# Mamba2 scan and SiLU MLP on one core: the second product of the first units in seven segments, and the sums of g's blocks moved from GpSimd to DMA and VectorE

## The chip, the cores and the metric

The kernel runs on one core of a Trainium2 chip. The metric is device time in microseconds (us) of one execution; the median of eight runs is what a change is judged by. A profile of one execution is at hand, with every instruction of every engine.

## The reference, cut to what matters

The inputs are `x` (4, 8, 768, 32), `a` (4, 8, 768), `B` and `C` (4, 8, 768, 16), and the weights `w_in` (256, 2048) and `w_out` (2048, 256), all float32.

```python
# block 1, for each batch and head: a state-space scan
y[i] = sum over j <= i of (C_i . B_j) * exp(cum_i - cum_j) * x_j + (C_i . state) * decay_i
# bridge: (batch, head, seq, dim) -> (3072 tokens, 256)
X = y.transpose(0, 2, 1, 3).reshape(3072, 256)
# block 2
h = X @ w_in          # (3072, 2048)
g = h * sigmoid(h)    # SiLU
out = g @ w_out       # (3072, 256)
```

The two large products, `X @ w_in` (the first) and `g @ w_out` (the second), hold most of the arithmetic.

## The kernel before, in words

The 3072 tokens are cut in 12 units of 256 tokens, three for each batch. For each unit the scan makes a transposed X (tile `XM`), the first product and SiLU make `g` (tile `gT`, 128 partitions x 16 blocks x 256 tokens, four buffers in `gpool`), and the second product reads `g` and `w_out`. All products are float32, and each 128x128 by 128x256 product is two TensorE instructions in the trace. There is no scheduler: engines carry out their instructions in the order in which the code emits them, and that order is written out by hand.

Two ways of doing the products stand side by side.

- Units 0 to 3 do the first product plainly: `f_s1(g, j)`, called for j = 0 to 7, makes two of the 16 blocks of `g` by four products and one SiLU on ScalarE.
- From unit 4 on, units are taken in pairs (`G` = 2 to 5, units 2G and 2G + 1), and `f_x1(G, j, ...)` does the first product of the pair with seven products in place of eight, the Strassen-Winograd way. It needs sums of blocks of `w_in` (`f_SW`, four tiles, each from one instruction on GpSimd) and sums of blocks of X (`f_XT`, four for each pair, on GpSimd).

The second product likewise. `s2_list` does it plainly for units 0 and 1: 64 products, with `g` as the weights that TensorE holds. `s2_pair(P)` does pairs 1 to 5 in seven segments of eight products, called "1", "w", "5", "6", "7", "4" and "3" and done in that order. Pair P's `g` is four blocks: b11 and b21 are the even and the odd blocks of unit 2P, b12 and b22 those of unit 2P + 1. Each segment accumulates in a PSUM tile `o_ps`, of which there is one buffer (`ps_o`, bufs=1); ScalarE copies it to a tile `ps` (`ppool`, five buffers), GpSimd adds such tiles (`p_add`), VectorE transposes the sum and SyncE's queue writes it out (`f_out`, called a round later through the list `PEND`). In the last pair VectorE takes GpSimd's additions, and every other segment uses a buffer of `hp` instead.

Segments "5", "6", "7" and "4" need sums of blocks: `f_TS(P, i, ...)` makes TN = b12 - b11 (in a tile of its own), then in place b11 = b22 - TN, b12 = b22 - b12 and b21 = b21 - b11. All are on GpSimd, in instructions of 128x256, other than two of the four sums of the last pair. `f_SO` makes the sums of blocks of `w_out` on VectorE.

`f_s2(n)` emits the next n products of the second product, whichever unit or pair they belong to. It is called between the products of the first one, so that the two alternate on TensorE: four products of each in turn in units 2 and 3, and from unit 4 on one "s" of the string `ORDER[j]` at a time, for example

```python
ORDER = ("W15s6sss7sss43", "W1s56ss7sss43s", ...
```

The scan of later units is emitted in between by `scan_piece` (pieces T, E, B, C, D, G, S, Y; S is `f_SW`) and by `scan_plan`. Piece G ends in small products on TensorE (`f_D0`, `f_G0`) followed by VectorE's `f_S` and `f_M` and ScalarE's `f_SM`; piece Y is further small products (`f_Y`) and ScalarE's copy of them to `XM` (`f_X`).

At the start the arriving weights are worked over in pieces (`w_size` on ScalarE, `w_bits` on VectorE and GpSimd; pieces b13 to b15 fall in unit 2), and `busy(n, small)` has TensorE multiply zeros, n products of 512 columns and `small` products of 64 columns.

Of the kernel before, what the change touches and what calls it, by code (L numbers as in the profile page):

```python
# [21 lines left out]
def kernel(  # L22
# [219 lines left out]
    busy(4, 14)  # L242
# [230 lines left out]


    def f_s1(g, j):
        if j == 0:
            GTS[g] = gpool.tile([128, NF, UT], FP32, name="gT")
        xm = XM[g].rearrange("p (w c) t -> p w (c t)", w=2)
        hp = ps_h.tile([128, 2, UT], FP32, name="hp")
        for i in range(2):  # L480
            f = 2 * j + i
            for kc in range(KC):
                nc.tensor.matmul(out=hp[:, i], lhsT=w_in_sb[:, kc, f * 128:(f + 1) * 128],  # L483
                                 rhs=xm[:, kc], start=(kc == 0), stop=(kc == KC - 1))
        nc.scalar.activation(GTS[g][:, 2 * j:2 * j + 2], hp, AF.Silu)  # L485
        if j == 7:
            XM.pop(g)


    def s2_list(units):  # L490
        for g in units:
            b, t0 = at(g)
            r = out[b * S + t0:b * S + t0 + UT].rearrange("(k c i) m -> k i c m", k=2, c=2)
            o = ps_o.tile([128, 2, d_model], FP32, name="o_ps")
            for c in range(2):
                for f in range(NF):
                    nc.tensor.matmul(out=o[:, c], lhsT=GTS[g][:, f, 128 * c:128 * c + 128], rhs=w_out_sb[:, f, :],  # L497
                                     start=(f == 0), stop=(f == NF - 1), skip_group_check=True)
                    if f == NF - 1 and c == 1:
                        for e in range(2):  # L500
                            o_sb = ppool.tile([128, UT], FP32, name="ps")
                            nc.scalar.activation(o_sb, o[:, e], AF.Copy)
                            for k in range(2):
                                nc.sync.dma_start(out=r[k][:, e], in_=o_sb[64 * k:64 * k + 64])
                    yield

# [3 lines left out]
    SO, TN, PEND = [], {}, []  # L510

    def f_SO(i):

        def lo(t):
            return t[:, 0:4], t[:, 4:8]

        def new():
            if i == 3:
                return lo(spare(None, 128))
            return [wtp.tile([128, 2, WF], FP32, name=n).rearrange("p a (b m) -> p (a b) m", m=128)  # L520
                    for n in ("wu", "wv")]

        SO.append(new())
        b = lambda k, m: lo(wjo[:, k, m])
        a0, a1, op = ((b(0, 1), b(1, 1), ALU.add), (SO[0], b(0, 0), ALU.subtract),
                      (b(0, 0), b(0, 1), ALU.subtract), (b(1, 0), SO[min(i, 1)], ALU.subtract))[i]
        for e in range(2):
            nc.vector.tensor_tensor(out=SO[i][e], in0=a0[e], in1=a1[e], op=op)

    def gb(P, k, v):  # L530

        return GTS[2 * P + v].rearrange("p (j k) t -> p k j t", k=2)[:, k]

    def f_TS(P, i, q, engine):


        if i == 0 and q == 0:
            TN[P] = tpool.tile([128, NF // 2, UT], FP32, name="TN")
        b11, b21, b12, b22 = gb(P, 0, 0), gb(P, 1, 0), gb(P, 0, 1), gb(P, 1, 1)
        o, a0, a1 = ((TN[P], b12, b11), (b11, b22, TN[P]), (b12, b22, b12), (b21, b21, b11))[i]  # L540
        for j in (2 * q, 2 * q + 1):
            engine.tensor_tensor(out=o[:, j], in0=a0[:, j], in1=a1[:, j], op=ALU.subtract)  # L542

    def p_add(o, p, q, engine):
        engine.tensor_tensor(out=o, in0=p, in1=q, op=ALU.add)  # L545
# [13 lines left out]
    def s2_pair(P, final=False):  # L559
# [3 lines left out]
                ("5", lambda j: SO[0][j // 4][:, j % 4], lambda: TN[P]),  # L563
                ("6", lambda j: SO[1][j // 4][:, j % 4], lambda: gb(P, 0, 0)),
                ("7", lambda j: SO[2][j // 4][:, j % 4], lambda: gb(P, 0, 1)),
                ("4", lambda j: wjo[:, 1, 1, j], lambda: gb(P, 1, 0)),
                ("3", lambda j: SO[3][j // 4][:, j % 4], lambda: gb(P, 1, 1)))
        for n, (m, w, g) in enumerate(segs):
            if final and n % 2 == 0:
                o = ps_h.tile([128, 2, UT], FP32, name="hp")[:, 0]  # L570
            else:
                o = ps_o.tile([128, 2, UT], FP32, name="o_ps")[:, 0]
            for j in range(NF // 2):
                nc.tensor.matmul(out=o, lhsT=w(j), rhs=g()[:, j], start=(j == 0), stop=(j == NF // 2 - 1))  # L574
                if j == NF // 2 - 1:

                    p[m] = ppool.tile([128, UT], FP32, name="ps")
                    on = o.rearrange("p (c k t) -> p c k t", c=2, k=2)
                    pn = p[m].rearrange("p (k c t) -> p c k t", c=2, k=2)
                    if not (final and m == "3"):  # L580
                        nc.scalar.activation(pn, on, AF.Copy)  # L581
                    if m == "w":
                        p_add(p["w"], p["w"], p["1"], adder)
                        PEND.append(partial(f_out, P, 0, 0, p["w"]))
                    elif m == "6":
                        p_add(p["6"], p["6"], p["1"], adder)
                    elif m == "7":
                        p_add(p["7"], p["7"], p["6"], adder)
                        p_add(p["6"], p["6"], p["5"], adder)
                        p_add(p["5"], p["5"], p["7"], adder)  # L590
                        PEND.append(partial(f_out, P, 1, 1, p["5"]))
                    elif m == "4":
                        p_add(p["4"], p["4"], p["7"], adder)
                        PEND.append(partial(f_out, P, 1, 0, p["4"]))
                    elif m == "3" and final:

                        for k in range(2):
                            nc.vector.tensor_tensor(out=pn[:, :, k], in0=on[:, :, k],
                                                    in1=p["6"].rearrange("p (k c t) -> p c k t", c=2, k=2)[:, :, k],
                                                    op=ALU.add)  # L600
                            f_out(P, 0, 1, p["3"], (nc.sync, nc.scalar), (128 * k, 128 * k + 128))
                    elif m == "3":
                        p_add(p["3"], p["3"], p["6"], adder)
                        PEND.append(partial(f_out, P, 0, 1, p["3"]))
                yield
# [17 lines left out]
    def f_SW(i):  # L623
# [5 lines left out]
        nc.gpsimd.tensor_tensor(out=t, in0=a0, in1=a1, op=op)  # L629
# [17 lines left out]
    def f_x1(G, j, dve, act):  # L647
        u0, u1 = 2 * G, 2 * G + 1
        if j == 0:
            for u in (u0, u1):  # L650
                GTS[u] = gpool.tile([128, NF, UT], FP32, name="gT")
# [23 lines left out]
        for what in ORDER[j]:  # L675
# [5 lines left out]
            elif what == "1":  # L681
                mm(X, wj[:, 0, 0, j], b0[:, 0])
                p1 = copy("p1", X)
                add(g0[:, 2 * j], W, p1)
# [4 lines left out]
            elif what == "6":  # L689
                mm(X, SW[1][:, j], t[:, 1], False)  # L690
                u2 = copy("u2", X)
                silu(g0[:, 2 * j], g0[:, 2 * j])
                other(dve, first)
            elif what == "7":
                mm(X, SW[2][:, j], t[:, 2], False)
                add(g1[:, 2 * j + 1], X, p5)
                silu(g1[:, 2 * j + 1], g1[:, 2 * j + 1])
            elif what == "4":
                mm(X, wj[:, 1, 1, j], t[:, 3], False)
                silu(g0[:, 2 * j + 1], X)  # L700
                other(dve, 2)
            elif what == "3":
                mm(Y, SW[3][:, j], b1[:, 1], False)
                add(g1[:, 2 * j], Y, u2)
                silu(g1[:, 2 * j], g1[:, 2 * j])
# [66 lines left out]
    busy(0, 24)  # L772
    f_G0(0)
    busy(4, 10)
# [14 lines left out]
    busy(3, 30)  # L789
# [47 lines left out]
    S2.append(s2_list((0, 1)))  # L837
    for j in range(8):
        f_s1(2, j)
        scan_piece(3, j, ("", "", "T", "E", "BS", "G", "S", "Y"))  # L840
        f_s2(4)
        if j < len(late):
            w_steps(late[j])
        if j in (2, 5):
            load_unit(4 + j // 3)

    def sums(P, qs):

        for q in qs:
            f_TS(P, 0, q, nc.gpsimd)  # L850
            f_TS(P, 2, q, nc.gpsimd)

    for j in range(8):
        f_s1(3, j)
        scan_piece(4, j, ("TE", "BS", "G", "Y", "", "", "", ""))
        scan_piece(5, j, ("", "", "T", "E", "BS", "G", "Y", ""))
        scan_piece(6, j, ("",) * 7 + ("t",))
        f_s2(4)
        if j in (2, 5):
            load_unit(6 + j // 3)  # L860
        if j in (1, 4, 6, 7):
            f_SO(len(SO))
# [3 lines left out]
        if j == 5:  # L866
            sums(1, (0, 1))
    for G in range(2, NU // 2):
# [3 lines left out]
        for j, (dve, act, pe) in enumerate(plan):  # L872
# [4 lines left out]
            for what in waiting:  # L877
                what()

            if j == 1:  # L880
                sums(G - 1, (2, 3) if G == 2 else (3,))
            if j == 1 or j == 4:
                for q in range(4):
                    f_TS(G - 1, (1, 3)[j // 4], q, nc.gpsimd)
# [3 lines left out]
            sums(G, {4: (0, 1), 6: (2,)}.get(j, ()))  # L888
# [3 lines left out]
    sums(P, (3,))  # L892
    S2.append(s2_pair(P, True))
    for n in range(7):
        f_s2(8)
        for what in PEND:
            what()
        PEND[:] = []
        if n in (0, 1):
            for q in range(4):  # L900
                f_TS(P, 2 * n + 1, q, nc.vector)
# [31 lines left out]
```

## Time and profile before

| what | value |
|---|---|
| median of 8 runs | 358.38 us (356.47 to 359.07) |
| the profiled execution: its time | 358.20 us |
| its span, first to last instruction | 356.4 us |
| TensorE products, busy | 346.9 us (97% of the span) |
| VectorE, ScalarE, GpSimd, busy | 183.1, 160.5 and 181.7 us |
| granted TensorE clock, mean | 0.996 |
| DMA | 26.53 MB in 110059 packets, 98884 of them under 512 bytes |

The profiled execution took 1.8 us more than its span, and 0.2 us less than the median. PE is TensorE's products, PEld its loading of weights, DVE is VectorE, ACT ScalarE, POOL GpSimd and SP SyncE; L574 is line 574 of the kernel. Busy time of PE is modelled: products overlap in a pipeline, so a line of eight products with 1.89 us in the timeline is followed 1.73 us after its start by the next.

### The profile page before, as it was taken

To read this page: it belongs to the slowest core of one execution; us is meant where nothing else is said; L and a number is where in the kernel's file an instruction comes from. 1 tells how busy PE (TensorE), PEld (TensorE's weight loads), DVE (VectorE), ACT (ScalarE), POOL (GpSimd) and SP (SyncE) were. 2 spreads that over 40 slices of the span, in tenths; PEclk is the share of its full clock that TensorE was granted. 3 is DMA by queue.
4 is the path that set the end of the run, shared out by engine and by line. 5 is a ranking of instruction groups with operands and counts; after the bars stand their busy time and mean duration, and the time that the engine had idled before them with its cause. 6 is when DMAs were issued, how large, how long until landed. Compare 5 with 4: busy or idle time off the path is not lost.

```text
span 356.4 us, 8461 instructions
## 1 busy us (share of the span) xinstructions
PE 346.9 (97%) x3352; PEld 291.9 (82%) x3353; DVE 183.1 (51%) x389; ACT 160.5 (45%) x390; POOL 181.7 (51%) x246
## 2 busy tenths in 40 slices
PE   7989999999999999999999999999999999999994
PEld 4568888888888888888888888888888888888883
DVE  6988989554447444633454633455632221214722
ACT  2559576223222545545544545544545454453100
POOL 3344345534059076498274398264398930596100
PEclk9999999999999999999999999999999999999998
DMA  6899957863654251161026152110101100101203
GB/s 115 214 348 139 329 167 123 128 118 61 119 105 63 66 88 26 45 110 27 15 61 105 41 96 44 17 16 2 17 2 16 17 15 0 17 0 21 41 0 45
DMA packets 110059, 26.53 MB, mean 74 GB/s; under 512 B 98884, under 2 KB 105796, under 8 KB 110020
## 3 DMA queue, kind: packets, MB, share of 16 engines
q1 hardware_dynamic: 107044, 25.67, 35.6%
q10 hardware_dynamic: 2976, 0.33, 0.6%
q8 instruction: 26, 0.43, 0.5%
q14 instruction: 13, 0.11, 0.1%
HBM read 22.83 MB, written 3.15 MB: 73 GB/s over the span
## 4 chain that ended last, share of the span: by engine, by line
PE 91%; DVE 4%; DMA 2%; issue 1%; POOL 0%; SPq 0%; ACT 0%; ACTq 0%; DVEq 0%
PE o_ps L574 30%; PE hp L657 28%; PE hp L483 15%; PE o_ps L497 8%; PE hp L574 3%; PE gy L463 2%; PE gy L454 2%; PE gy L400 2%; DVE E L299 1%; PE gy L385 1%; DMA tbc<-in_C_dram 1%; DVE wv L178 1%; DMA tbc<-in_B_dram 1%; DMA out_dram<-ot 0%; DVE gT L275 0%
## 5 line engine op out<-in xcount | busy, mean ns | idle before, releaser
L660 DVE TENSOR_TENSOR gT<-hp,p 128x256 f32<-128x256 f32 x64 | 26.9, 420 | 84.6 <-ACT p L671 47.4
L483 PE MATMUL hp<-XM,w_in_sb 128*128 128x256 f32 x256 | 59.4, 381 | 1.6 <-POOL w_in_sb L182 0.9
L663 ACT ACTIVATE gT<-gT 128x256 f32<-128x256 f32 x96 | 39.7, 414 | 42.8 <-DVE gT L660 42.8
L336 POOL TENSOR_TENSOR BT<-bn,E 128x256 f32<-128x256 f32 x12 | 8.9, 741 | 95.6 <-PE hp L657 29.7
L574 PE MATMUL o_ps<-gT,w_out_sb 128*128 128x256 f32 x224 | 56.5, 379 | 0.0
L483 PEld LDWEIGHTS hp<-XM,w_in_sb 128*128 128x128 f32 x256 | 48.1, 190 | 9.3 <-POOL w_in_sb L182 2.0
L657 PE MATMUL hp<-raw 128*128 128x256 f32 x192 | 52.7, 380 | 0.0
L542 POOL TENSOR_TENSOR gT<-gT 128x256 f32<-128x256 f32 x72 | 51.2, 741 | 0.0
L574 PEld LDWEIGHTS o_ps<-gT,w_out_sb 128*128 128x128 f32 x224 | 42.4, 190 | 5.9
L657 PEld LDWEIGHTS hp<-raw 128*128 128x128 f32 x192 | 36.2, 190 | 5.4 <-POOL ps L545 0.6
L485 ACT ACTIVATE gT<-hp 128x512 f32<-128x512 f32 x32 | 19.1, 596 | 39.7 <-PE hp L483 39.6
L671 ACT ACTIVATE p<-hp 128x256 f32<-128x256 f32 x64 | 24.5, 384 | 27.5 <-PE hp L657 25.7
L660 DVE TENSOR_TENSOR gT<-hp,u 128x256 f32<-128x256 f32 x32 | 13.6, 424 | 40.8 <-PE hp L657 40.8
L657 PE MATMUL hp<-XM,w_in_sb 128*128 128x256 f32 x128 | 34.1, 389 | 0.0
L545 POOL TENSOR_TENSOR ps<-ps 128x256 f32<-128x256 f32 x28 | 20.3, 728 | 26.1 <-ACT ps L581 12.8
L497 PE MATMUL o_ps<-w_out_sb,gT 128*128 128x256 f32 x128 | 30.9, 384 | 0.0
L542 POOL TENSOR_TENSOR TN<-gT 128x256 f32<-128x256 f32 x40 | 28.7, 740 | 0.0
L497 PEld LDWEIGHTS o_ps<-w_out_sb,gT 128*128 128x128 f32 x128 | 23.8, 190 | 3.8 <-issue 0.5
L657 PEld LDWEIGHTS hp<-XM,w_in_sb 128*128 128x128 f32 x128 | 23.3, 190 | 4.3 <-issue 1.0
L299 DVE TENSOR_TENSOR_SCAN E<-ab,diag 128x256 f32<-128x256 f32 (+1 forms) x32 | 24.5, 804 | 3.7 <-PE gy L463 3.4
L542 POOL TENSOR_TENSOR gT<-gT,TN 128x256 f32<-128x256 f32 x32 | 22.2, 733 | 0.0
L581 ACT ACTIVATE ps<-o_ps 128x256 f32<-128x256 f32 x31 | 11.9, 383 | 18.5 <-PE o_ps L574 18.2
(123 smaller groups left out, 548.5 us busy)
## 6 DMA issues: line engine op xcount, KB each, us to landing
ab<-in_a_dram SPq DMA_DIRECT2D x40, 128.0 KB, 3.5
raw<-in_moe_w_in_dram SPq DMA_DIRECT2D x8, 512.0 KB, 8.2
raw<-in_moe_w_out_dram SPq DMA_DIRECT2D x8, 512.0 KB, 6.7
xt<-in_x_dram SPq DMA_DIRECT2D x24, 128.0 KB, 4.2
out_dram<-ot SPq DMA_DIRECT2D x76, 32.0 KB, 1.7
bn<-in_B_dram SPq DMA_DIRECT2D x22, 64.0 KB, 5.0
tbc<-in_C_dram SPq DMA_DIRECT2D x40, 32.0 KB, 1.9
pa<-in_a_dram SPq DMA_DIRECT2D x10, 128.0 KB
```

The costliest lines, as they stand in the source:

```text
L299: nc.vector.tensor_tensor_scan(out=E[u].rearrange("p k h t -> p (k h t)")[:, Q * g0:Q * (g0 + n)], data0=t.rearrange("p g t -> p (g t)"), ...
L483: nc.tensor.matmul(out=hp[:, i], lhsT=w_in_sb[:, kc, f * 128:(f + 1) * 128], rhs=xm[:, kc], start=(kc == 0), stop=(kc == KC - 1))
L485: nc.scalar.activation(GTS[g][:, 2 * j:2 * j + 2], hp, AF.Silu)
L497: nc.tensor.matmul(out=o[:, c], lhsT=GTS[g][:, f, 128 * c:128 * c + 128], rhs=w_out_sb[:, f, :], start=(f == 0), stop=(f == NF - 1), skip_ ...
L542: engine.tensor_tensor(out=o[:, j], in0=a0[:, j], in1=a1[:, j], op=ALU.subtract)
L545: engine.tensor_tensor(out=o, in0=p, in1=q, op=ALU.add)
L574: nc.tensor.matmul(out=o, lhsT=w(j), rhs=g()[:, j], start=(j == 0), stop=(j == NF // 2 - 1))
L581: nc.scalar.activation(pn, on, AF.Copy)
L657: nc.tensor.matmul(out=o, lhsT=w, rhs=x_, start=start, stop=True, skip_group_check=True)
L660: nc.vector.tensor_tensor(out=o, in0=p, in1=q, op=ALU.add)
L663: nc.scalar.activation(o, i, AF.Silu)
L671: nc.scalar.activation(o, i, AF.Copy)
```

## The change

- Units 0 and 1 become pair 0 of `s2_pair`; `s2_list` goes. With `joint=True` the segments "1" and "w" of pair 0 are done together in the two halves of one `o_ps` tile, alternating, 16 products; the other five follow one by one. The loop of unit 2 calls `f_s2(2)` for j = 0 and 1 and `f_s2(4)` after, that of unit 3 calls `f_s2(4 - j % 2)`: 28 products each, 56 together, where it was 64.
- Signs are turned so that all four sums of blocks of `g` are additions: TN = b12 + b11, b12 += b22, b11 += b12, b21 += b11. The segments' order becomes "1", "w", "5", "7", "6", "4", "3".
- `f_T1` makes TN on VectorE, in instructions of 128x512. The other three are made by `f_TS` as accumulating DMAs from GpSimd's queue, two of 128x1024 (512 KB) for each sum; in the last pair some are on GpSimd and VectorE, in instructions of 128x1024.
- `gT` is laid out so that each of the four blocks is contiguous in a partition.
- `f_SW` moves from GpSimd to VectorE. `f_SO` is called earlier (units 2 and 3), since pair 0 needs it.
- In the loop of unit 2, the scan piece is emitted after `f_s2`; the places of pieces move by a round.
- `busy` is called with other counts: 4 large and 14 small products become 5 large; 24 small become 20; 4 and 10 become 4 and 8; 3 and 30 become 4 and 17.

```diff
-    busy(4, 14)
+    busy(5)
...
+    def f_T1(P, q, engine=nc.vector):
+        if q == 0:
+            TN[P] = tpool.tile([128, NF // 2, UT], FP32, name="TN")
+        js = slice(2 * q, 2 * q + 2)
+        engine.tensor_tensor(out=TN[P][:, js], in0=gb(P, 0, 1)[:, js], in1=gb(P, 0, 0)[:, js], op=ALU.add)
...
+    def f_TS(P, i, h, engine=None):
+        b11, b21, b12, b22 = gb(P, 0, 0), gb(P, 1, 0), gb(P, 0, 1), gb(P, 1, 1)
+        js = slice(4 * h, 4 * h + 4)
+        o, a = {3: (b12, b22), 2: (b11, b12), 4: (b21, b11)}[i]
+        if engine is None:
+            nc.gpsimd.dma_start(out=o[:, js], in_=a[:, js], accum_op=ALU.add)
+        else:
+            engine.tensor_tensor(out=o[:, js], in0=a[:, js], in1=o[:, js], op=ALU.add)
...
+        if joint:
+            o = ps_o.tile([128, 2, UT], FP32, name="o_ps")
+            for j in range(NF // 2):
+                for n, (m, w, g) in enumerate(segs[:2]):
+                    nc.tensor.matmul(out=o[:, n], lhsT=w(j), rhs=g()[:, j], start=(j == 0 and n == 0), ...)
+                    if j == last and n == 1:
+                        end("1", o[:, 0])
+                        end("w", o[:, 1])
+                    yield
...
-        nc.gpsimd.tensor_tensor(out=t, in0=a0, in1=a1, op=op)      # f_SW
+        nc.vector.tensor_tensor(out=t, in0=a0, in1=a1, op=op)
...
-    S2.append(s2_list((0, 1)))
+    S2.append(s2_pair(0, joint=True))
     for j in range(8):
+        waiting, PEND[:] = PEND[:], []
         f_s1(2, j)
-        scan_piece(3, j, ("", "", "T", "E", "BS", "G", "S", "Y"))
-        f_s2(4)
+        f_s2(2 if j < 2 else 4)
         if j < len(late):
             w_steps(late[j])
+        if j == 2:
+            scan_piece(3, 0, "T")
+            for q in range(4):
+                f_T1(0, q)
+        if j == 3:
+            f_SO(0)
+        scan_piece(3, j, ("", "", "", "E", "DC", "", "G", "Y"))
+        if j in (5, 6):
+            f_SO((2, 1)[j - 5])
+        outputs(waiting)
...
+        for h in range(2):
+            if j in (3, 5, 7):
+                f_TS(0, {3: 3, 5: 2, 7: 4}[j], h)
     for j in range(8):
+        waiting, PEND[:] = PEND[:], []
         f_s1(3, j)
-        scan_piece(4, j, ("TE", "BS", "G", "Y", "", "", "", ""))
-        scan_piece(5, j, ("", "", "T", "E", "BS", "G", "Y", ""))
+        scan_piece(4, j, ("TE", "DCS", "G", "YS", "", "", "", ""))
+        scan_piece(5, j, ("", "", "T", "E", "DCS", "G", "YS", ""))
         scan_piece(6, j, ("",) * 7 + ("t",))
-        f_s2(4)
+        f_s2(4 - j % 2)
+        if j == 3:
+            f_SO(3)
+        outputs(waiting)
+        if j == 5:
+            f_T1(1, 0)
+            f_T1(1, 1)
+            f_TS(1, 3, 0)
...
         if j == 7:
             for i in range(4):
                 f_XT(2, i)
...
+            if j == 0:                     # in the loop of f_x1(G, j)
+                f_T1(G - 1, 2)
+                f_T1(G - 1, 3)
+                f_TS(G - 1, 3, 1)
+            if j == 1 or j == 3:
+                for h in range(2):
+                    f_TS(G - 1, {1: 2, 3: 4}[j], h)
+            if j == 5:
+                f_T1(G, 0)
+                f_T1(G, 1)
+                f_TS(G, 3, 0)
```

## The prediction

> **What bounds the kernel now.** I read the page's busy time and slices first, then TensorE's waits, then the timelines of single engines around the places that the change touches.
>
> ```profile
> PE 346.9 (97%) x3352; PEld 291.9 (82%) x3353; DVE 183.1 (51%) x389; ACT 160.5 (45%) x390; POOL 181.7 (51%) x246
> ...
> PE   7989999999999999999999999999999999999994
> ...
> PEclk9999999999999999999999999999999999999998
> DMA  6899957863654251161026152110101100101203
> ```
>
> TensorE (PE) is full from the third slice to the last but one, at full clock. All its waits:
>
> ```profile
> PE o_ps L221 <- DVE gT L216: 1.3, 1, 1.3
> PE hp L483 <- POOL w_in_sb L182: 0.9, 1, 0.9
> PE hp L483 <- ACT XM L472: 0.7, 1, 0.7
> PE gy L400 <- ACT ce L361: 0.7, 1, 0.7
> PE gy L454 <- issue: 0.5, 1, 0.5
> ```
>
> They lie before 28 us. From there to 348 us the time is the number of products; a product removed there is time, and so is every new wait of PE. The price of a product, from the chain that ended last: sixteen instructions, one segment, 3.45 us.
>
> ```profile
> 327.40 3.45 PE hp L574 x16
> ```
>
> That is 0.216 us for an instruction, 0.43 for a product. GpSimd (POOL), half busy, never holds PE up in this stretch, so relieving it brings nothing by itself.
>
> **Part 1, fewer products.** Units 0 and 1 took 64 products (L497), pair 0 takes 56: 8 x 0.43 = **-3.45 us**, all on the path.
>
> **Part 2, three new waits.** These come from where PE's steps fall. There is one `o_ps` buffer, so a segment's first product waits for ScalarE's copy of the segment before. In `ORDER` a first-product step stands at each such seam, and so does `f_s1` at most seams of pair 0. Counting its steps (units 2 and 3: 2, 2, 4, 4, 4, 4, 4, 4, 4, 3, 4, 3, 4, 3, 4, 3), segments end after steps 16, 24, 32, 40, 48. Steps 16, 24 and 32 end a call. Step 40 is the first of three in unit 3's j = 3, step 48 the second of three in j = 5: there "4" and "3" follow straight on. What ScalarE has before the copy is seen at the same place of before (unit 3, after Y of unit 4 and after G of unit 5):
>
> ```profile
> 98.66 1.99 PE L497 MATMUL o_ps<-w_out_sb,gT 128*128 128x256 f32 x8
> ...
> 106.75 1.99 PE L497 MATMUL o_ps<-w_out_sb,gT 128*128 128x256 f32 x8
> ```
> ```profile
> 98.77 0.60 ACT L472 ACTIVATE XM<-gy 128x512 f32<-128x512 f32 x1
> ...
> 107.93 0.69 ACT L434 ACTIVATE sm<-st,par 128x128 f32<-128x128 f32 x2 [1.46 <-DVE st L426]
> ...
> 117.29 0.66 ACT L502 ACTIVATE ps<-o_ps 128x256 f32<-128x256 f32 x2 [1.13 <-PE o_ps L497]
> ```
>
> Seam at step 40: PE's step runs 98.66 to 99.09; ScalarE's queue has XM until 99.37, then the copy (0.38, L581's mean) until 99.77; PE goes on at 99.82 (0.05 for the hand-over, as between XM and L483): **+0.73**. Seam at step 48: two steps, 106.75 to 107.61, but the copy stands behind the two `sm` that wait for VectorE's states, until 108.62; copy to 109.02, PE at 109.07: **+1.46**. Bounds for each: 0.62 if ScalarE is free (0.16 of pipeline after the last product, 0.03, 0.38, 0.05), and the values above.
>
> The third is at the end of unit 3. There the last product ends "3", GpSimd has to add its copy, and only behind that in its queue stand the four `f_XT` that `f_x1(2, 0)` reads. Before, no addition stood ahead of them, and all four were done when PE got there:
>
> ```profile
> 114.60 0.74 POOL L640 TENSOR_TENSOR raw<-XM 128x256 f32<-128x256 f32 x1
> 115.29 0.73 POOL L640 TENSOR_TENSOR raw<-XM,raw 128x256 f32<-128x256 f32 x1
> ```
>
> With before's clock: last product out at 117.25, copy 117.29 to 117.67, addition 0.73 (L545), first XT 0.76, so 119.2; PE, after "W" and "1", wants it at 117.96: **+1.29** (up to 1.9 with XTs of 0.91 and 1.07, as two of before were). Later XTs keep ahead of PE. Sum: 0.73 + 1.46 + 1.29 = **+3.48**. The three waits eat the eight products.
>
> **Part 3, the sums.** All 102 us of L542 on GpSimd go (51.2 + 28.7 + 22.2), off the path: gain nothing. `f_T1` puts two 128x512 on VectorE twice a pair, 0.67 each alone (L528's quickest) to 1.23 beside GpSimd. From pair 1 on VectorE is busy 25 of 54 us a stage, and the delay of 1.3 to 2.5 falls after round 0, behind which L660's addition has one round until PE writes its buffer again: nothing. For pair 0, VectorE runs without a break from b15's end (62.8): T 1.3, TN 2.7, `f_SO(0)` 1.4, so "5" can start at 68.2 and PE reaches it at 70.7; E takes 4.0 more and BT 0.74, 73 against G at 75.9. Nothing, with 2.5 us to spare; 3.3 us more, if all six ran beside GpSimd, would cost up to 1.
>
> `f_SW` on VectorE: four times 1.3 to 2.5 (twice L528) in rounds where VectorE was idle; behind them wait only states that PE's G releases later. Without that cover up to 1.2 each. `f_SO` only moves. SyncE's queue gets 16 writes of 32 KB in place of 8 of 64 KB, ahead of the loads of units 5 and 6, which start some 5 us later and are read some 10 us after they land: nothing. L581's five extra copies replace L502's four.
>
> The accumulating DMAs appear in no row of before. Each is 512 KB, two to a sum, and for pair 0 the three sums are a chain: GpSimd's queue issues b11 += b12 only when the half of b12 has landed, and b21 += b11 likewise, with unit 4's BT behind. Issue can begin when TN ends, 62.8 + 1.3 + 2.7 = 66.8. When are they wanted? Unit 2's products begin at 53.43 in before; its rounds are 2.59 twice and 3.45 six times, with G (1.0) and Y (1.3): 81.6. Unit 3: 3.45, 3.02, then G at 89.8; with G, Y and the seam of step 40, step 44 falls at 100.2. That is when the last half of the third sum is wanted, 66.8 + 3 sums, and G wants BT (0.74) behind two: by both a sum may take **11.1 us**. From pair 1 on the tightest is b21, issued after j = 3 and wanted 12.5 us later (half of it; the rest 3 us after).
>
> What does a sum take? Nearest rows:
>
> ```profile
> raw<-in_moe_w_out_dram SPq DMA_DIRECT2D x8, 512.0 KB, 6.7
> ...
> out_dram<-ot SPq DMA_DIRECT2D x76, 32.0 KB, 1.7
> ```
>
> Low end: both source and target are read, 2.1 MB at the page's fastest slice (348 GB/s) is 6.0, plus 1.7 of landing: 7.7. High end: two halves one after another at the slowest load of this size (8.2): 16.4. I take 10, nearer the low end since the DMA engines are 0.57 busy in units 2 and 3 and so have room: hidden, **0**. At 16.4: 3 x 5.3 in pair 0 and 2 to 4 in each of four pairs, some +27.
>
> The Trainium skill, "DMA: Bandwidth & Descriptors", section "Anatomy of one DMA", fits 2.0 us plus bytes at 436 GB/s: by it a sum, with its double reading, would be an estimated 6.8 us, hidden too. A rule that speaks against the change is in "SBUF — State Buffer", section "Who interferes with whom": VectorE's two-port instructions lock GpSimd out, and GpSimd then can't write descriptors for its DMAs. The trace has the lock in the other direction:
>
> ```profile
> 49.30 0.43 DVE L176 TENSOR_SCALAR wu<-wu 128x512 uint32<-128x512 uint32 x1
> ...
> 50.70 1.38 DVE L176 TENSOR_SCALAR wu<-wu 128x512 uint32<-128x512 uint32 x1
> ```
>
> The second ran beside GpSimd's L182 (50.41 to 51.79), the first alone. By that rule each issue could be put off by an instruction such as L317 (0.67); three such in the chain are 2 us, less than the slack either way.
>
> **Part 4, products of zeros.** The chain of the start runs through the load of C, VectorE's E, M and weights, up to L182 at 22.8; PE's zeros stand in its gaps. Nothing, other than 0.55 us of "issue" at 25.07 and 0.22 at 15.25, where PE waits for no one in the midst of many short instructions; 62 instructions fewer ahead of them may shorten it. I take half of the first, **-0.25** (bounds -0.75 and +0.3). The clock may fall if zeros leave a gap: the longest grows from 0.66 to some 0.8 us; unlikely.
>
> **Tail.** The last pair keeps 7 x 3.45; its sums are ready (TN at 330 against 334.2, b12 by GpSimd, 4 x 0.74, at 333.5 against 337.6). Nothing.
>
> **Sum.** 358.20 - 3.45 + 3.48 - 0.25 = 357.98 for an execution like the profiled one; the median of runs stands 0.2 above: **358.2 us**.
>
> **Rivals.** *The gain arrives.* The waits shrink to the free-ScalarE price, 0.62 + 0.62, and the XT wait is shorter since the addition slips through: 358.4 - 3.45 + 1.5 - 0.5 = 356.0; with no waits at all 354.5. Against: the queue orders are written in the code. *The sums land late* (the slower side): a sum of more than 11.1 us, since accumulation reads twice and pair 0 works beside two units' loads (DMA share 0.57 in units 2 and 3). PE then stands at "6", "4" or G of unit 4, three times the excess: at 12.6 us +4.5, so 362.6, at 16.4 some 385. Against: the free half of the DMA engines, and a share of 0.07 to 0.34 in the later stages. *The change doesn't do what it says* would need the 64 products to stay; the code emits 56, and PE's count must fall by 47 (16, and 31 zeros). I give that no chance.
>
> **How the numbers follow.** A measurement tells 0.3% (1.07 us) from no change. Waits eat the gain, 356.8 to 359.2: 0.50; of it 0.13 faster, 0.32 the same, 0.05 slower. The gain arrives, 354.5 to 357.3: 0.23, 0.22 faster. Sums late: 0.27, nearly all slower, four tenths of it under 362.6. Faster 0.35, same 0.33, slower 0.32. The range leaves out the gain's best end and the sums' worse six tenths: 355.2 to 362.6.
>
> **What would show it.** PE waits at the seams, "PE o_ps <- ACT ps" twice, 0.7 and 1.5, and "hp <- POOL raw" once, 1.3, all between 95 and 119 us; none for a DMA. PE's share stays 97%. If PE waits on `gT` for a DMA, the sums are late. If PE has no waits at all after 28 us, part 2 is wrong, and the time near 355.

## The result, and the profile after

The changed kernel takes 360.15 us (median of 11 runs, 359.77 to 361.18), the kernel before 357.42 us (32 runs, 356.47 to 359.10): a ratio of 1.0073, 95% interval 1.0058 to 1.0089, so 2.6 us slower. The forecast was 358.2 us, no measurable change, in a range of 355.2 to 362.6; what came is a loss of 0.7%, clear of the noise. The profiled execution took 360.57 us, with a span of 358.9 us. From the page of the changed kernel:

```profile
PE 344.2 (96%) x3305; PEld 287.0 (80%) x3306; DVE 207.0 (58%) x409; ACT 162.0 (45%) x393; POOL 111.9 (31%) x137
...
PEclk9999999999999999999999999999999999999999
...
L535 POOL DMA_DIRECT2D gT<-gT x31 | 27.1, 883 | 75.2 <-issue 19.1
...
gT<-gT POOLq DMA_DIRECT2D x31, 512.0 KB, 6.0
```

TensorE (PE) has 47 instructions and 2.7 us of work less, GpSimd (POOL) 70 us, and the accumulating DMAs land 6.0 us after their issue (median; 4.5 to 8.0). Most of the time went into waits of PE. TensorE's waits in the changed kernel, all four that lie behind the start (in all, times, longest, in us; one of the two on `XM` lies in the start, as before):

```profile
PE o_ps L614 <- ACT ps L571: 1.6, 2, 1.1
PE hp L487 <- ACT XM L472: 1.4, 2, 0.7
...
PE hp L669 <- POOL raw L652: 1.2, 1, 1.2
PE hp L669 <- DVE gT L672: 1.1, 3, 0.4
```

Their places, in the timeline of TensorE (start, length, and in brackets the idle time with its releaser):

```profile
82.00 1.99 PE L487 MATMUL hp<-XM,w_in_sb 128*128 128x256 f32 x8 [0.69 <-ACT XM L472]
...
97.64 1.13 PE L614 MATMUL o_ps<-gT,w_out_sb 128*128 128x256 f32 x4 [0.47 <-ACT ps L571]
...
107.11 0.70 PE L614 MATMUL o_ps<-gT,raw 128*128 128x256 f32 x2 [1.11 <-ACT ps L571]
...
117.92 0.48 PE L669 MATMUL hp<-raw 128*128 128x256 f32 x1 [1.17 <-POOL raw L652]
...
128.48 0.70 PE L669 MATMUL hp<-raw,w_in_sb 128*128 128x256 f32 x2 [0.36 <-DVE gT L672]
```

The idle time in brackets is less than the delay, because products overlap. With 0.216 us for an instruction, the four ahead of the row at 107.11 started at 104.86 and would have let it start at 105.72: 1.39 us of delay. In the same way the others are 0.74 (97.64), 1.33 (117.92) and 0.62 (128.48, with the slower product behind it). The last comes back at 183.01 and 237.52.

To compare kernels I cut each profiled execution at four marks that all of them have: the second group of `o_ps<-ident,bn` transpositions (unit 2's), the first product of pair 2's `f_x1`, the last unit's Y (its second group of products, `gy<-E,xt`), and PE's last product. From the last Y to PE's last product every kernel takes 85.7 us, so that column is left out.

| kernel | start, to the 1st mark | units 2 and 3 | pairs, to the last Y | tail | span |
|---|---|---|---|---|---|
| before | 41.7 | 75.41 | 148.76 | 4.83 | 356.4 |
| after | 40.9 | 74.84 | 152.07 | 5.38 | 358.9 |
| after, T1 on GpSimd in the pairs | 40.7 | 74.84 | 150.19 | 5.66 | 357.1 |
| after, sums by GpSimd instead of DMA | 40.6 | 74.84 | 161.44 | 5.39 | 368.0 |
| after, Y of unit 3 ahead of `f_s2` | 45.4 | 74.86 | 152.08 | 5.38 | 363.4 |
| after, counts 4,4,4,4,4,4,2,2 | 43.5 | 72.71 | 152.07 | 5.63 | 359.6 |
| after, XT first | 40.9 | 74.85 | 150.63 | 5.33 | 357.4 |
| after, G and Y a step earlier | 42.6 | 74.34 | 152.07 | 5.53 | 360.3 |
| after, p5's output first | 40.4 | 74.84 | 152.08 | 5.26 | 358.3 |
| after, the same, SP and ACT in turn | 40.0 | 74.85 | 152.06 | 5.25 | 357.9 |
| before, new counts of zeros | 42.7 | 75.41 | 148.76 | 4.91 | 357.5 |
| after, all repairs | 41.1 | 72.19 | 148.96 | 4.92 | 352.9 |
| after, all repairs, SP and ACT in turn | 40.3 | 72.20 | 148.97 | 4.94 | 352.1 |

Unchanged parts repeat to 0.02 us from one kernel to the next, so a difference of a tenth of a microsecond in the two middle columns is readable from one profile each. The start is not of that kind: it moves by up to 5 us between kernels that are the same there. The medians are no finer: the kernel before, run again beside each group of experiments, had medians from 356.77 to 357.75 us. So what a single repair is worth is read from the two middle columns; its median shows it only in part.

From before to after: start -0.8, units 2 and 3 -0.6, pairs +3.3, tail +0.55: +2.5 us of span.

### The profile page after: what moved, and what is told of

Read it like the earlier page. It is cut to its first block, busy times and chain, and to the rows that moved or that the text cites. A ratio compares the mean times of both kernels' runs of the same rounds, so it can differ in the third digit from the quotient of the medians.

```text
span 358.9 us, 8348 instructions
## 1 busy us (share of the span) xinstructions
PE 344.2 (96%) x3305; PEld 287.0 (80%) x3306; DVE 207.0 (58%) x409; ACT 162.0 (45%) x393; POOL 111.9 (31%) x137
## 4 chain that ended last, share of the span: by engine, by line
PE 76%; DVE 10%; SPq 7%; DMA 3%; issue 2%; POOL 1%; ACT 0%; ACTq 0%; DVEq 0%
PE o_ps L614 28%; PE hp L669 26%; PE hp L487 11%; DVE E L299 4%; PE hp L614 4%; SPq L115 2%; PE gy L463 2%; PE o_ps L600 2%; SPq L122 2%; PE gy L454 1%; DMA tbc<-in_B_dram 1%; SPq L549 1%; PE gy L400 1%; DVE TN L526 1%; SPq L95 1%
## 5 line engine op out<-in xcount | busy, mean ns | idle before, releaser
L672 DVE TENSOR_TENSOR gT<-hp,p 128x256 f32<-128x256 f32 x64 | 26.9, 420 | 78.4 <-ACT p L683 42.2
L614 PE MATMUL o_ps<-gT,w_out_sb 128*128 128x256 f32 x240 | 60.7, 380 | 0.5 <-ACT ps L571 0.5
L540 POOL TENSOR_TENSOR ps<-ps 128x256 f32<-128x256 f32 x35 | 29.4, 841 | 81.7 <-ACT ps L571 80.4
L614 PEld LDWEIGHTS o_ps<-gT,w_out_sb 128*128 128x128 f32 x240 | 45.4, 190 | 7.2 <-ACT ps L571 0.9
L535 POOL DMA_DIRECT2D gT<-gT x31 | 27.1, 883 | 75.2 <-issue 19.1
L672 DVE TENSOR_TENSOR gT<-hp,u 128x256 f32<-128x256 f32 x32 | 13.6, 424 | 39.3 <-PE hp L669 39.3
L299 DVE TENSOR_TENSOR_SCAN E<-ab,diag 128x256 f32<-128x256 f32 (+1 forms) x32 | 25.8, 845 | 0.4
L571 ACT ACTIVATE ps<-o_ps 128x256 f32<-128x256 f32 x38 | 14.4, 382 | 22.3 <-PE o_ps L614 20.6
L614 PE MATMUL o_ps<-gT,wu 128*128 128x256 f32 x88 | 22.4, 380 | 0.0
L614 PE MATMUL o_ps<-gT,wv 128*128 128x256 f32 x88 | 22.4, 380 | 0.0
L614 PE MATMUL o_ps<-gT,raw 128*128 128x256 f32 x80 | 20.6, 382 | 1.1 <-ACT ps L571 1.1
L669 PE MATMUL hp<-raw,w_in_sb 128*128 128x256 f32 x64 | 19.4, 384 | 1.1 <-DVE gT L672 1.1
```

Of the source, the lines that this page charges most:

```text
L299: nc.vector.tensor_tensor_scan(out=E[u].rearrange("p k h t -> p (k h t)")[:, Q * g0:Q * (g0 + n)], data0=t.rearrange("p g t -> p (g t)"), ...
L535: nc.gpsimd.dma_start(out=o[:, js], in_=a[:, js], accum_op=ALU.add)
L540: engine.tensor_tensor(out=o, in0=p, in1=q, op=op)
L669: nc.tensor.matmul(out=o, lhsT=w, rhs=x_, start=start, stop=True, skip_group_check=True)
L672: nc.vector.tensor_tensor(out=o, in0=p, in1=q, op=ALU.add)
```

## Experiments

The theory after the comparison of the two traces: the eight products did come off, and six separate delays, each with a cause of its own in the written order, cost more than they brought: two seams, the XT wait, the `XM` wait, TN on VectorE (three times), all five of PE, and behind PE's last product the last pair's additions. The rivals: the waits are one effect that moves on when it is taken away; and the DMA sums cost the later stages by what they do to memory or queues.

**TN by GpSimd in the pair loop.**

```diff
-                f_T1(G - 1, 2)
-                f_T1(G - 1, 3)
+                f_T1(G - 1, 2, nc.gpsimd)
+                f_T1(G - 1, 3, nc.gpsimd)
```

> The changed kernel, with one edit: in the loop of the pairs, the second half of TN (the f_T1 calls after round 0) is made by GpSimd in place of VectorE. Theory A (VectorE's TN delays L672's additions of round 1, and TensorE's product "4" waits for them, 0.62 us in each of three stages): TensorE's waits "hp <- DVE gT L672" vanish, and the time falls by 1.9 us, from 360.15 to about 358.2. Rival B (the stages lose time to the accumulating DMAs, by lateness or by their load on the DMA engines): the DMAs are the same, so the time stays at 360.1 within 0.4.

358.88 us, ratio to before 1.0057 (1.0032 to 1.0082), less of a gain than the 1.9 us expected, and not clear of the changed kernel's interval. In the profile the pairs took 1.88 us less and PE's three waits on L672 are gone. VectorE's timeline shows how they arose. Before, in round 1 of pair 2's stage, with PE's product "4" of that round behind it:

```profile
124.93 0.40 DVE L660 TENSOR_TENSOR gT<-hp,p 128x256 f32<-128x256 f32 x1
125.24 1.26 DVE L299 TENSOR_TENSOR_SCAN E<-ab,diag 128x256 f32<-128x256 f32 x2
126.79 0.42 DVE L660 TENSOR_TENSOR gT<-hp,p 128x256 f32<-128x256 f32 x1 [0.28 <-PE hp L657]
```
```profile
127.88 0.59 PE L657 MATMUL hp<-raw,w_in_sb 128*128 128x256 f32 x2
```

And after:

```profile
125.00 0.42 DVE L547 STREAM_TRANSPOSE ot<-ps 128x256 f32<-128x256 f32 x1
125.34 1.25 DVE L526 TENSOR_TENSOR TN<-gT 128x512 f32<-128x512 f32 x2
126.51 0.42 DVE L672 TENSOR_TENSOR gT<-hp,p 128x256 f32<-128x256 f32 x1
126.84 1.26 DVE L299 TENSOR_TENSOR_SCAN E<-ab,diag 128x256 f32<-128x256 f32 x2
128.02 0.40 DVE L672 TENSOR_TENSOR gT<-hp,p 128x256 f32<-128x256 f32 x1
```

The second addition reads the buffer that product "7" has filled, and product "4" of the same round adds into that buffer, only three second products (`sss`) after "7". Before, there were some 0.9 us of slack: the addition was itself waiting for PE (0.28), and it ended 0.67 ahead of "4", of which the hand-over takes 0.06. Now T1 (1.17 to the next start) and the transposition of an output (0.34) stand ahead of it, 1.5 us together. The addition starts at 128.02 instead of 126.79, and "4" at 128.48, 0.53 us later than the products ahead of it would have let it. The transposition alone, which stays in this run, fits into the slack.

**The other sums by GpSimd instead of DMA, pairs 1 to 4.**

```diff
-                f_TS(G - 1, 3, 1)
+                f_TS(G - 1, 3, 1, nc.gpsimd)
...
-                    f_TS(G - 1, {1: 2, 3: 4}[j], h)
+                    f_TS(G - 1, {1: 2, 3: 4}[j], h, nc.gpsimd)
...
-                f_TS(G, 3, 0)
+                f_TS(G, 3, 0, nc.gpsimd)
```

> The changed kernel, with the three sums of b12, b11 and b21 of pairs 1 to 4 made by GpSimd in instructions of 128x1024 in place of accumulating DMAs (pair 0 keeps its DMAs, VectorE keeps TN). Theory A (VectorE's TN is what costs the later stages): 360.1, no faster, at most 1 us slower where GpSimd's additions hold up VectorE's. Rival B (the DMAs cost the later stages): about 1.9 us faster, 358.2.

370.67 us, ratio 1.0384 (1.0345 to 1.0423): 9.4 us more in the pairs than the changed kernel. Neither theory expected that; theory A allowed 1 us. It shows that sums in this form are no way to do without the DMAs. That the DMAs themselves cost these stages next to nothing is shown by the kernel with all repairs below: with the same DMAs its pairs take 148.96 us, against 148.76 before. GpSimd's, VectorE's and TensorE's timelines of this kernel:

```profile
126.40 2.34 POOL L537 TENSOR_TENSOR gT<-gT 128x1024 f32<-128x1024 f32 x1 [6.22 <-DVE TN L526]
```
```profile
126.57 3.31 DVE L299 TENSOR_TENSOR_SCAN E<-ab,diag 128x256 f32<-128x256 f32 x2
```
```profile
130.24 0.70 PE L669 MATMUL hp<-raw,w_in_sb 128*128 128x256 f32 x2 [2.40 <-DVE gT L672]
```

Two scans that take 1.26 us stand 3.31 beside one addition of GpSimd, and the same addition of L672 comes 2 us later still. That delay (some 2.0 us beyond the changed kernel's 0.62) comes three times, 6.1 us. The rest is the clock: after the second and the third wait (2.46 us each) the windows of the trace show a mean granted clock (the column behind POOL's) of 0.62 over four microseconds, then 0.95 over four; after the first (2.40 us) it stayed at 1.00.

```profile
186.00:190.00 4.00, 3.12 (x26) 2.12 (x30) 1.25 (x3) 1.22 (x3) 3.35 (x3) 0.62 0.24 65
190.00:194.00 4.00, 4.00 (x70) 3.33 (x51) 1.44 (x5) 1.34 (x4) 3.13 (x3) 0.95 1.03 154
...
244.00:248.00 4.00, 2.95 (x14) 1.94 (x22) 1.42 (x4) 1.11 (x3) 3.19 (x3) 0.62 0.02 4
```

Four microseconds at 0.62 and four at 0.95 lose 1.7 us, twice 3.4: together some 9.5 us, about the 9.4 measured.

**Y of unit 3 ahead of the second products, as it stood before.**

```diff
+        if j == 7:
+            scan_piece(3, 0, "Y")
         f_s2(2 if j < 2 else 4)
...
-        scan_piece(3, j, ("", "", "", "E", "DC", "", "G", "Y"))
+        scan_piece(3, j, ("", "", "", "E", "DC", "", "G", ""))
```

> The changed kernel, with piece Y of unit 3 emitted ahead of f_s2 in unit 2's last round, as it was in the kernel before. Theory: f_s1(3, 0) no longer follows Y directly, so its wait for ScalarE's copy to XM (0.69 us at 82.0) is covered by f_s2's four products: -0.7 us, 359.4. Against it: the time is made up by a later wait in unit 3 (the seams stay), then 360.1.

362.11 us, ratio 1.0136 (1.0093 to 1.0178), but units 2 and 3 took what they took in the changed kernel. The wait on `XM` is gone and another of the same length stands in its place, at Y itself:

```profile
83.47 0.58 PE L454 MATMUL gy<-cw,sm 32*64 32x64 f32 x24 [0.70 <-ACT gT L489]
```

G stands at the end of the round before, so only one call of `f_s1` (four products) is left between G and Y. Here the rival is right: this wait moves. The longer time of the profile (365.1 us, the slowest of its six runs) lies in the start, where nothing was edited:

```profile
27.03 0.94 PE L463 MATMUL gy<-E,xt 64*32 64x64 f32 x60 [1.64 <-issue]
28.66 4.63 PE L487 MATMUL hp<-XM,w_in_sb 128*128 128x256 f32 x10 [0.69 <-ACT XM L472]
```
```profile
28.00:32.00 4.00, 3.34 (x8) 2.71 (x9) 2.68 (x5) 2.84 (x5) 1.09 (x1) 0.50 0.79 122
```

PE stopped for 1.64 us after 4 of 64 small products with nothing to wait for that the profile shows, and the mean clock of the next slice was 0.50.

**G and Y of unit 3 a step earlier.**

```diff
-        scan_piece(3, j, ("", "", "", "E", "DC", "", "G", "Y"))
+        scan_piece(3, j, ("", "", "", "E", "DC", "G", "Y", ""))
```

> The changed kernel, with pieces G and Y of unit 3 a round earlier (j = 5 and 6). With Y alone moved ahead of f_s2 the wait for XM went and one of the same length came at Y, since only f_s1 stood between G and Y. Theory: with a whole round between G and Y and another between Y and f_s1(3, 0), both waits go, and from unit 1's transposes to the end the profile is 0.7 us shorter (317.3 in place of 318.0). Against it: G a round earlier waits for BT of unit 3, and nothing is won.

Units 2 and 3 took 0.50 us less: the wait on `XM` (0.69) gives way to one of 0.2 at G on `BT`. So most of this one can be had, with a whole round (eight products) between G and Y. The median, 360.68 us (ratio 1.0089, 1.0056 to 1.0122), does not show it; in this kernel's profile (362.03 us, the slowest of its four runs) the start took 1.7 us longer.

**Unit 3's second products in steps of 4, 4, 4, 4, 4, 4, 2, 2 instead of 4, 3, 4, 3, ...** (28 as before, but no segment ends within a call).

```diff
-        f_s2(4 - j % 2)
+        f_s2(4 if j < 6 else 2)
```

> The changed kernel, with unit 3's calls of f_s2 at 4, 4, 4, 4, 4, 4, 2, 2 products in place of 4, 3, 4, 3, 4, 3, 4, 3, so that segments end at the end of a call and f_s1 stands at each seam. Theory: the two waits "o_ps <- ACT ps" (0.74 and 1.39 us with the time until the next product) vanish, -2.1 us, 358.0. Against it: the sums by DMA for pair 0 are wanted sooner and come late, then TensorE waits for a DMA at segment "4" and little is won.

359.17 us, ratio 1.0058 (1.0033 to 1.0083), units 2 and 3 2.13 us less: both seams (0.74 and 1.39) are gone, and a first product stands at each. The 358.0 us expected were not reached; in the profile (361.31 us, the slowest of its runs) the start took 2.6 us longer, with a stop of PE of 1.57 us in the same 64 small products and a mean clock of 0.61 in the slice after. TensorE's timeline at the place of the first:

```profile
99.47 1.99 PE L614 MATMUL o_ps<-gT,w_out_sb 128*128 128x256 f32 x8
101.31 1.89 PE L487 MATMUL hp<-XM,w_in_sb 128*128 128x256 f32 x8
```

**XT emitted ahead of the last second products of unit 3.**

```diff
+        if j == 7:
+            for i in range(4):
+                f_XT(2, i)
         f_s2(4 - j % 2)
...
-        if j == 7:
-            for i in range(4):
-                f_XT(2, i)
```

> The changed kernel, with the four f_XT of pair 2 emitted before f_s2 in unit 3's last round, so that they stand ahead of the addition of segment "3" in GpSimd's queue. Theory: TensorE's wait "hp <- POOL raw L652" (1.33 us until the next product) vanishes, and from unit 1's transposes to the end the profile is 1.3 us shorter (316.7 in place of 318.0). Against it: VectorE's first additions of pair 2 take its place, and less than half is won.

359.06 us, ratio 1.0028 (1.0002 to 1.0054), the pairs 1.44 us less. The product that waited 1.17 us now follows without a gap:

```profile
116.58 0.59 PE L669 MATMUL hp<-raw 128*128 128x256 f32 x2
```

**The kernel before with the new counts of zeros alone.**

```diff
-    busy(4, 14)
+    busy(5)
...
-    busy(0, 24)
+    busy(0, 20)
...
-    busy(4, 10)
+    busy(4, 8)
...
-    busy(3, 30)
+    busy(4, 17)
```

> The kernel before, with nothing but the changed kernel's counts of products of zeros (5, 20, 4 and 8, 4 and 17). Theory A (the changed kernel's start, 0.8 us earlier in its profile, comes from fewer short instructions ahead of the "issue" waits): 0.8 us faster than before. Rival B (the start varies from execution to execution by more than that, whatever the zeros): no difference within 0.5.

357.22 us, ratio 0.999 (0.9968 to 1.0011): no difference, and the parts after the start are those of before to 0.01 us.

**The output of p5 ahead of the subtraction that makes p6, last pair only** (three additions ahead of the transposition instead of four, p6 made after "4").

```diff
-                p_add(p["6"], p["5"], p["6"], adder, ALU.subtract)
-                p_add(p["5"], p["5"], p["7"], adder, ALU.subtract)
-                PEND.append(partial(f_out, P, 1, 1, p["5"]))
+                if final:
+                    p_add(p["1"], p["5"], p["7"], adder, ALU.subtract)
+                    PEND.append(partial(f_out, P, 1, 1, p["1"]))
+                else:
+                    ...
```

> The changed kernel; in the last pair alone the sum that is written out after segment "6" is made before the one that is kept (three additions of VectorE ahead of its transposition, as before, in place of four). Theory: what lies behind TensorE's last product falls from 5.4 us to the 4.8 of before. Rival: the tail is longer for another reason, and stays at 5.4.

360.21 us, ratio 1.007 (1.0045 to 1.0094): no gain that the median can show, 0.12 us of the tail in the profile. The 4.8 us expected for the tail were not reached. The chain as it was supposed is seen in the two traces. VectorE and SyncE's queue (SPq), before:

```profile
345.12 1.34 DVE L545 TENSOR_TENSOR ps<-ps 128x256 f32<-128x256 f32 x3 [2.97 <-ACT ps L581]
```
```profile
346.96 7.05 SPq L554 DMA_DIRECT2D out_dram<-ot  x12
```

After:

```profile
347.11 1.80 DVE L540 TENSOR_TENSOR ps<-ps 128x256 f32<-128x256 f32 x4 [7.26 <-ACT ps L571]
```
```profile
349.42 7.19 SPq L549 DMA_DIRECT2D out_dram<-ot  x12
```

PE's last product ends at 351.57 and 353.52. Measured from it, SP's twelve issues begin 4.61 us ahead of it before and 4.10 ahead after, and end 2.44 and 3.09 behind it. With p5's output first they begin 4.55 ahead and end 2.75 behind.

**The same, and the outputs of p5 and "4" of the last pair issued by SP and ACT in turn.**

```diff
-                    PEND.append(partial(f_out, P, 1, 1, p["1"]))
+                    PEND.append(partial(f_out, P, 1, 1, p["1"], (nc.sync, nc.scalar)))
...
-                PEND.append(partial(f_out, P, 1, 0, p["4"]))
+                PEND.append(partial(f_out, P, 1, 0, p["4"], (nc.sync, nc.scalar) if final else None))
```

> Of the last pair alone: three additions instead of four stand before the transposition of p5 (as in the run before this one), and the outputs of p5 and of "4" are issued by SP and ACT in turn, not by SP alone. Theory (SP's twelve issues, 7.2 us in a row, and the two ot buffers set the tail of the changed kernel): the first half's transposition starts without its 0.28 us of idle time and the tail from PE's last product to the end of the span goes from 5.38 to 4.8 us, the median 0.5 us below the changed kernel. Rival (the tail is set by the time that the last outputs take to land): the tail stays at 5.3 us.

360.12 us, ratio 1.007 (1.0046 to 1.0094), tail 5.25: the theory of the queue failed, and the idle 0.27 us ahead of the first half's transposition stayed. Over all profiles the tail is 5.33 to 5.66 us in the seven kernels with four additions at that place, 4.92 to 5.26 in the four with three, and 4.83 and 4.91 in the two with before's order. The means of the two groups lie some 0.4 us apart, but the two profiles that differ by this edit alone lie 0.12 apart, and kernels that agree in the last pair differ by 0.3 (5.26 and 4.92). So the fourth addition is not shown to be the cause; what made the tail 0.55 us longer stays open.

**All repairs together** (TN on GpSimd, unit 3's counts, XT first, G and Y a step earlier, p5's output first).

> The changed kernel with all the repairs tried alone: T1(G-1,2) and T1(G-1,3) on GpSimd, second products 4,4,4,4,4,4,2,2 in unit 3's steps, XT ahead of the second products at step 48, G and Y of unit 3 a step earlier, p5's output ahead of p6's subtraction in the last pair. If the costs add up (theory: they are separate waits of PE): 1.88 + 2.13 + 1.4 + 0.4 + 0.1 = 5.9 us less than the changed kernel, from the mark 312.1 us instead of 318.0 (before: 314.7), a median of 354.2 us, ratio to before 0.991. Rival (PE's waits only move on to the next buffer): less than half of that, a median over 357 us.

354.56 us, ratio to before 0.9919 (0.9897 to 0.9940): 2.9 us faster than before and 5.6 faster than the changed kernel. Units 2 and 3 fell by 2.65 (2.13 + 0.50 expected), the pairs by 3.11 (1.88 + 1.44), the tail by 0.46. All of PE's waits behind the start:

```profile
PE gy L385 <- POOL BT L336: 0.2, 1, 0.2
```

**All repairs, with the outputs of the last pair by SP and ACT in turn.** The edit is the one shown above.

> The kernel with all the repairs, and in the last pair the outputs of p5 and "4" issued by SP and ACT in turn. Theory: 0.5 us below the kernel with all the repairs, a median of 353.7 us. Rival: no difference.

354.06 us, ratio 0.9916 (0.9883 to 0.9948), tail 4.94 against 4.92: no difference between the two. Both beat both kernels.

## Why the prediction was right and wrong, by its steps

- **Part 1, -3.45 us:** right. With all but one of the waits gone, units 2 and 3 take 72.19 us against 75.41, 3.22 less, with 0.2 of wait left.
- **Part 2, +3.48 us:** right to a tenth. Forecast 0.73, 1.46 and 1.29; measured 0.74, 1.39 and 1.33 by the timeline, and each is returned when its cause is taken away (2.13 for the two seams, 1.44 for XT).
- **Part 2 was not complete.** It looked at steps that changed their count and not at those that changed places with each other. In the last round of unit 2, Y moved behind `f_s2`, so the copy to `XM` lost the 1.73 us of second products that had hidden it: 0.69 us, of which 0.50 could be had back.
- **Part 3, VectorE: this is the step that failed most.** "Behind which L660's addition has one round until PE writes its buffer again: nothing". The cover that it named is not there. PE writes the buffer of the second addition again not a round later, but at "4" of the same round, three second products (1.3 us) behind "7"; the string `"W1s56ss7sss43s"` says so. The two T1 stand in VectorE's queue ahead of an addition, two scans and this second addition, whose slack was some 0.9 us before; a transposition takes 0.34 of it, and T1 is 1.17. The cost was 0.62 in each of three stages, 1.9 us, and it went when TN went to GpSimd. A low share (25 of 54 us) says nothing about the slack at one place of an in-order queue.
- **Part 3, the DMA sums: right, near the size assumed.** PE waits for none. One DMA of 512 KB, half a sum, took 6.0 us from issue to landing. A whole sum can be read for b11 of pair 0, where the next sum's issues wait for its halves:

```profile
73.29 0.86 POOL L535 DMA_DIRECT2D gT<-gT  x1
74.41 0.85 POOL L535 DMA_DIRECT2D gT<-gT  x1 [0.26 <-issue]
78.62 0.85 POOL L535 DMA_DIRECT2D gT<-gT  x1 [3.36 <-DMA gT<-gT]
82.51 0.86 POOL L535 DMA_DIRECT2D gT<-gT  x1 [3.04 <-DMA gT<-gT]
```

From the first issue (73.29) to the release of the last (82.51) that is 9.2 us, against the 10 taken and the 11.1 allowed. The estimate of 6.8 us that the prediction took from the Trainium skill, "DMA: Bandwidth & Descriptors", section "Anatomy of one DMA", is below that. The rival that the sums land late has no row to stand on. That relieving GpSimd brings nothing was right too: the pairs took 148.76 us with its 102 us of additions, in instructions of 128x256, and 148.96 with all repairs, where most of them are gone.
- **Part 3, a miscount without effect:** pair 0 brings seven copies of `o_ps` to ScalarE, not five (38 in place of 31 on L571 and L581), since the two halves of the joint tile are copied singly. No wait beyond those of part 2 comes from them.
- **Part 4, -0.25 us:** nothing is shown (ratio 0.999). The start was 0.8 us shorter in the changed kernel's profile, but it differs by more than that between kernels that agree there.
- **Tail, "Nothing":** wrong by 0.55 in the two profiles. The prediction asked only whether the sums are ready. The order of "6" and "7" puts a fourth addition ahead of an output, but taking it out gave back 0.12, and a second queue for the outputs nothing; the cause stays open.

With the two missed terms and the tail, the sum would have been 357.98 + 1.9 + 0.7 + 0.55 = 361.1, and 360.6 with the start as it came out in that profile; it took 360.57. The rival "the gain arrives" had put 354.5 on a kernel with no waits at all, and the kernel with the waits repaired took 354.56. That the two agree so closely is in part luck: the rival reckoned from a kernel before of 358.4 us, and beside the repaired kernel it took 357.41, so the gain was 2.9 us and not 3.9.

## What to carry to other kernels

Where PE is full, go through each engine's queue at each place where an instruction is inserted or changes places, and read the slack of the next thing that PE waits for in that row, up to the product that needs it; an engine's mean share does not give it. Where a gain vanishes into waits, price each by the product that it holds up: here they were separate and added up, and moving four pieces of the written order, and TN back to GpSimd, made a loss of 0.7% a gain of 0.8%. A wait that sits between two fixed neighbours can move instead (Y for `XM`), so try a move that adds work between them.

## What the runs showed of the hardware that was not expected

- One GpSimd addition of 128x1024 (2.34 us) held up two VectorE scans with two inputs in SBUF for most of its length (3.31 us instead of 1.26). The Trainium skill, "SBUF — State Buffer", section "Who interferes with whom", has a VectorE instruction with two SBUF inputs contend with GpSimd's reads; these rows agree. The same work by DMA leaves the scans at 1.26.
- Stops of PE of 1.64 and 2.46 us were followed by a mean granted clock of 0.50 and 0.62 over the next slice of 4 us, one of 2.40 us was not. Nor does the length of one stop decide it at the start: one of 0.87 us (G and Y a step earlier) was followed by 0.70, one of 1.03 (all repairs) by 1.00, both with the same 0.69 us wait on `XM` behind them, and with waits on `w_in_sb` of 0.94 and 0.51 some microseconds ahead. The Trainium skill, "TensorE: Matmul & The Clock Gate", section "What's actually happening", has the clock halved after at least one idle window of some 3.4 us; in these runs shorter stops were followed by a lower clock, and a wait of 2.5 us cost up to 4. What decides it was not tried.
- In the midst of 64 small products of the start PE stopped for between 0 and 1.64 us without any wait that the profile shows, at the same line (L463) and after the fourth of them in nine of the thirteen profiles. What sets its length was not tried.
